# Memories a batch ahead, in the scores' visit, and turned by VectorE and a trip through HBM

## The chip, the cores and the metric

The kernel runs on one core of a Trainium2 chip. The metric is the time of one execution on the device in microseconds (us), as the median of several runs; lower is better.

## What is computed

An attention with 32 memories a head, followed by a bilinear feed-forward network, for 8 batches (0 to 7) of 8 heads, 576 positions and 64 channels. All data is float32.

```python
a = phi - max(phi, over positions)            # phi: [b, h, 576, 32]
a = exp(a); a = a / (sum(a, over positions) + 1e-9)
k_m = einsum('bhsm,bhsd->bhmd', a, k)         # the memories of the keys
v_m = einsum('bhsm,bhsd->bhmd', a, v)         # and of the values
scores = matmul(q, k_m.T) / 8
attn = softmax(scores, over the 32 memories)
x = matmul(attn, v_m)                         # 4608 rows of 512
h = (x @ w1) * (x @ w2)                       # 1024 wide
out = (h @ w3) @ w_out
```

The kernel multiplies w3 by w_out once, and each batch's value memories by w1 and w2, so that x itself is never made.

## The kernel before, in words

After a start that loads and multiplies the weights, a loop runs over the batches. Each turn has two stages, and the order of the instructions on every engine is written out by hand: tables of step names, run by `go`, each name advancing a generator by one piece.

`ab_stage(b)`, the product stage, multiplies the attention of batch b by its weights, for eight blocks f of 128 columns. Its periods p are numbered 0 to 9: a period runs seven products of one block (names q1 to q7, three matmuls of 288 columns each) and the other engines' steps on them: copies on ScalarE, hold_c22, gr0, gr1 and the seeds on VectorE, `high` on ScalarE and `low` on GpSimd. VectorE's hold_c22 of a block must be done before its last product q4 starts. At the `+` of each period stand the steps that the table `MEETS` names, all for batch b + 1: the maximum over positions (`top`, `row`: the maxima go to HBM and come back spread over all partitions as the tile all), the exponentials with positions along the free axis (`exp`, for the sums), `norm` (two small steps on VectorE: add 1e-9, reciprocal), and `less`, which subtracts the maxima from phi laid out by rows (two long and two short additions on VectorE) and takes its exponential (two on ScalarE). At the `*` of period 8 come the memories (`mem`, L262): 40 small matmuls of those rows with keys and values (L270 and L279, 32 columns of the array each) into the PSUM pair x, and two scaled copies on ScalarE into kvm.

`out_stage(b)` runs the output blocks of batch b (24 matmuls of 512 columns each, in four groups of six, written O) and, between them by the table `REST`, the rest of batch b + 1: `blocks` (L293: two transposes on TensorE with ident, and VectorE's copy into the tile memory), the scores (`sc0`, `sc1`: 8 small matmuls each), M0 directly behind them, the softmax over memories (`se`, `sn`, `pr`), the sums of the attention's blocks (`ps`), and M3, M2, M1. M0 to M3 multiply memory by a quarter of w1 and w2 each (L387), and those quarters are read back from HBM (the DRAM tiles kept) by SP: W0 to x, W1 to the tile kv2, W2 to the tile q, W3 to the tile kv0. W1 and W3 can only be issued once the memories have read keys and values from these tiles, W2 once sc1 has read the queries. The loads of the next inputs (`phi2`, `rows2`, `q2`, `kv2`) follow M1.

SP issues every DMA, in order, and all go through one queue. TensorE, ScalarE, VectorE and GpSimd each run their own list in order.

Of the kernel before, what the change touches and what calls it, by code (L numbers as in the profile page):

```python
# [8 lines left out]
F32 = mybir.dt.float32  # L9
# [30 lines left out]
A11 A6 B3 A3 norm.1 A6 A10 C24 A6 A3 B10 A10 C24 S3 A3 A7 A3 N3 A7 A10 A10 B7 N3 A10 O0 A7 less.1 N3 A7 A2 A7 A15  # L40
less.1 less.1 A2 B15 A15 A14 less.1 A15 A15 B14 A15 less.1 B2 A13 A2 A14 mem.1 A2 A14 mem.1 X1 A13 X3 A2 A14 B13 A14
blocks.1 A12 A13 A13 blocks.1 B12 A13 A12 A12 A12 A12
""".split()
MEETS = {0: "<M3 top", 1: "top row exp", 2: "exp", 3: "norm", 4: "W0", 5: "less", 6: "less less less", 7: "less"}
REST0 = """
# [10 lines left out]
def memory_attention__then__bilinear_ffn_kernel(  # L56
# [67 lines left out]
    def pair():  # L124
        x = psum_pair()
        return [x[:, i] for i in range(2)]
# [13 lines left out]
    def whole(step):  # L140
        for _ in step:
            pass
# [45 lines left out]

    ready = {}

    def attention(b):

        v = {}
# [68 lines left out]
        def memories():  # L262
            kvt = loaded.pop(("kv", b))
            v["kvm"] = att.tile([P, NT, 2 * D], F32, name="kvm")

            ps = pair()
            for t in range(NT):
                for i in range(4):
                    for h in range(4):
                        nc.tensor.matmul(  # L270
                            ps[t][h * M : (h + 1) * M, : 2 * D],
                            lhsT=v["a"][:, i, t, h * M : (h + 1) * M],
                            rhs=kvt[i][:, (4 * t + h) * 2 * D : (4 * t + h + 1) * 2 * D],
                            start=i == 0,
                            stop=False,
                        )
            for h in range(4):
                for t in range(NT):
                    nc.tensor.matmul(  # L279
                        ps[t][h * M : (h + 1) * M, : 2 * D],  # L280
                        lhsT=v["a"][t * D : (t + 1) * D, 4, 0, h * M : (h + 1) * M],
                        rhs=kvt[4][t * D : (t + 1) * D, h * 2 * D : (h + 1) * 2 * D],
                        start=False,
                        stop=True,
                    )
            yield
            for t in range(NT):

                nc.scalar.activation(
                    out=v["kvm"][:, t], in_=ps[t][:, : 2 * D], func=AF.Copy, scale=v["sm"][:, t : t + 1]  # L290
                )

        def blocks():  # L293
# [3 lines left out]
            yield  # L297
            nc.vector.tensor_copy(out=memory[b % 2], in_=ps.rearrange("p (t g m) -> p t g m", t=NT, m=M))

        def scores(n, banks):  # L300

            if "q" not in v:
                v["q"] = loaded.pop(("q", b))
                s_sb = att.tile([P, 5 * NT * P], F32, name="s_sb", tag="a")
                v["s"] = s_sb[:, : NT * S].rearrange("p (n k m) -> p n k m", n=2, m=M)
            ps = [x[:, :HALF] for x in banks()]
            turned = n == 1 and b > 0
            for g in range(NG):
                for t in range(NT):
                    nc.tensor.matmul(  # L310
                        ps[t][g * M : (g + 1) * M],
                        lhsT=memory[b % 2][t * D : (t + 1) * D, t, g],
                        rhs=v["q"][t * D : (t + 1) * D, g, n * HALF : (n + 1) * HALF],
                        start=True,
                        stop=True,
                    )
            yield
            nb = NBLK // 2
            for t in range(NT):
                nc.vector.transpose(  # L320
                    out=v["s"][:, n, (t ^ turned) * nb :][:, :nb], in_=ps[t].rearrange("p (k m) -> p k m", m=M)
                )
# [45 lines left out]
                nc.gpsimd.tensor_tensor(out=lo[:, i:j], in0=y, in1=hi[:, i:j].bitcast(F32), op=ALU.subtract)  # L368
                yield

        steps = {"ps": sums, "top": top, "row": row, "less": less, "exp": exp, "norm": norm, "mem": memories, "blocks": blocks}
        steps |= {f"turn{i}": lambda i=i: turn(i) for i in (0, 4)}
        for n in range(2):
            steps |= {f"sc{n}": lambda n=n: scores(n, banks_aa if b and n else pair)}
# [53 lines left out]
    def memory_weights(b, q):  # L428
        ps = pair() if q == 3 else [psum(ps_ab, "bab"[q]) for _ in range(NT)]
        weights_times(b, q, w12_sb[0] if (b, q) == (1, 0) else staged[q], ps)  # L430
        (b12, b11), (b21, b22) = [[x[:, k * FQ : (k + 1) * FQ] for k in range(2)] for x in ps]
        yield
        if q == 2:
            x = const.tile([P, CW], F32, name="u", bufs=2).rearrange("p (k f) -> p k f", k=4)
        else:
            x = room_of_sums()[:, int(q == 1)]
        t1, t2, t3, t4 = [x[:, k] for k in range(4)]
        mh, ml = ready["M", b][q] = [new.tile([P, 7, FQ], F32R, name=f"{z}{q}") for z in ("mh", "ml")]
        firsts = ((0, 1, b11), (1, 3, ps[1].rearrange("p (k f) -> p k f", k=2)))
        nc.scalar.copy(out=t4, in_=b12)  # L440
        for i, j, y in firsts:
            nc.scalar.copy(out=mh[:, i:j], in_=y)
        yield
        for y, p, r in ((t1, t4, b11), (t3, b22, t4), (t2, b22, t1), (t4, b21, t2)):
            nc.vector.tensor_tensor(out=y, in0=p, in1=r, op=ALU.subtract)
        for i, j, y in firsts:
            nc.vector.tensor_tensor(out=ml[:, i:j], in0=y, in1=mh[:, i:j].bitcast(F32), op=ALU.subtract)
        yield
        nc.scalar.copy(out=mh[:, 3:], in_=x)  # L449
        for k in range(0, 4, 2):  # L450
            y = slice(3 + k, 5 + k)
            nc.gpsimd.tensor_tensor(out=ml[:, y], in0=x[:, k : k + 2], in1=mh[:, y].bitcast(F32), op=ALU.subtract)  # L452
# [196 lines left out]
    def ab_matmuls(b, n, f, w):  # L649
# [12 lines left out]
            )  # L662
        yield

    POOLF = (2, 3)

    def ab_unit(b, n, f):
# [89 lines left out]

    def ab_stage(b, go, before, part):
        u = [Sevenths(b, f) for f in range(NF)]
        order = """  # L760
            0q1 0q5 0seed_u 0keep_q5 / 2gr1 + 1q7 1q3 2high * 2low 1hold_c22 1gr0 0q6 0q2 0hold_c11 0seed_c 1q4
        """.split()
        for p in range(NF + 2):
            for x in order:
                if x == "+":
                    if p == NF and b + 1 < B:
                        started[b] = out_block(b, 0), 1
                        next(started[b][0])
                    for what in MEETS.get(p, "").split():
                        if what[0] == "<":  # L770
                            before(what[1:])
                        elif what[0] == "W":
                            if b + 1 < B:
                                whole(stage(int(what[1])))
                        else:
                            go(what)
                elif x == "*":
                    if p == NF:
                        go("mem")
                        go("mem")  # L780
                        if b + 1 == B:
                            started[b] = out_block(b, 0, psum_pair()[:, 0]), 1
                            next(started[b][0])
                elif x == "/":
                    if p == 0:
                        whole(part)
                elif 0 <= p - int(x[0]) < NF:
                    getattr(u[p - int(x[0])], x[1:])()
# [44 lines left out]
    def goer(b):  # L833
        begun = {x[:-2]: step for x, step in under_way.items() if b == 0 and x.endswith(".1")}

        def go(what):
            if b + 1 == B:
                return
            if what not in begun:
                if what[0] == "M":  # L840
                    begun[what] = memory_weights(b + 1, int(what[1]))
                else:
                    begun[what] = steps[b + 1][what]()
            next(begun[what], None)
            if what == "M0" and new is None:
                renew()

        return go
# [12 lines left out]
    def out_stage(b, go):  # L861
        ready["M", b + 1] = {}
        part, left = out_parts(b), 4 * ((S + b % 2 * REST_ROWS) // P)
        if b in started:
            left -= started[b][1]
        next(part)
        for what in (REST if b else REST0) + left * ["O"]:
            if what == "O":
                if left > (b + 1 < B):
                    left -= 1  # L870
                    next(part)
            elif what[:-1] in LOADS:
                whole(load(what, b))
            elif what[0] == "W":
                if b + 1 < B:
                    whole(stage(int(what[1])))
            else:
                go(what)
        return part
# [78 lines left out]
```

## Time and profile before

| | us |
|---|---|
| median of 3 runs (509.57 to 510.89) | 509.64 |
| the profiled execution | 509.37 |
| its span, first to last instruction | 507.6 |
| TensorE busy | 502.7 |
| VectorE busy | 356.4 |
| ScalarE busy | 295.9 |
| GpSimd busy | 192.8 |
| DMA queue, share of 16 engines | 52.5% |

The profile shows one execution. Busy times of different engines overlap; the busy time of TensorE counts matmuls whose ends overlap too. What counts is who waited for whom, and the chain of waits, which goes back from the last instruction through whatever released each step.

### The profile page before, as it was taken

What the parts mean: (1) busy time and instruction counts of PE and PEld (TensorE: products, weight loads), DVE (VectorE), ACT (ScalarE), POOL (GpSimd) and SP (SyncE); (2) the same over time, 40 slices, a digit from 0 to 9 for tenths busy, and PEclk for the clock granted to TensorE, in tenths of its full rate; (3) what the DMA queues carried; (4) which work ended last, traced back from release to release, by engine and by line L of the source; (5) the groups of instructions that cost most, each with busy time, mean ns of one, the idle gap of its engine ahead of it and who ended that gap; (6) DMA issues with size and microseconds to landing.
All of it is one profiled execution on the core that took longest, in us unless ns stands there. A gap on an engine that the chain in (4) does not pass through costs nothing.

```text
span 507.6 us, 10188 instructions
## 1 busy us (share of the span) xinstructions
PE 502.7 (99%) x3879; PEld 412.0 (81%) x3879; DVE 356.4 (70%) x741; ACT 295.9 (58%) x574; POOL 192.8 (38%) x137
## 2 busy tenths in 40 slices
PE   8999999999999999999999999999999999999997
PEld 6447688967986899769977899779977898689986
DVE  5889999598758847497749576697759474976400
ACT  7998977438653756267626465377635564475411
POOL 0000010027641744238532925168515644276500
PEclk9999999999999999999999999999999999999999
DMA  8999983979216931657246730776077522500011
GB/s 344 418 416 420 393 331 110 375 251 386 99 49 240 365 111 57 235 202 284 81 177 207 321 116 1 271 297 232 2 262 260 205 94 78 215 28 16 1 47 57
DMA packets 21680, 102.24 MB, mean 201 GB/s; under 512 B 2560, under 2 KB 3712, under 8 KB 12800
## 3 DMA queue, kind: packets, MB, share of 16 engines
q1 hardware_dynamic: 21632, 101.60, 52.5%
q8 instruction: 30, 0.49, 0.4%
q14 instruction: 18, 0.15, 0.1%
HBM read 87.95 MB, written 13.64 MB: 200 GB/s over the span
## 4 chain that ended last, share of the span: by engine, by line
PE 89%; DMA 5%; DVE 3%; ACT 1%; issue 1%; POOL 0%; POOLq 0%; ACTq 0%
PE o L803 38%; PE b L688 14%; PE a L688 9%; PE o L688 9%; DMA kv<-in_weights 5%; PE x L270 3%; PE a L569 3%; PE b L569 3%; PE b L387 3%; PE x L387 2%; PE x L635 1%; PE a L387 1%; PE x L803 1%; PE b L656 1%; PE x L310 1%; PE a L656 1%
## 5 line engine op out<-in xcount | busy, mean ns | idle before, releaser
L756 POOL TENSOR_TENSOR gl<-u,gh 128x576 fp32r<-128x576 f32 x56 | 80.0, 1428 | 97.8 <-ACT gh L753 82.3
L803 PE MATMUL o<-W,gh 128*128 128x512 f32 (+1 forms) x288 | 96.4, 389 | 0.0
L452 POOL TENSOR_TENSOR ml<-x,mh 128x512 fp32r<-128x512 f32 x42 | 58.4, 1424 | 83.0 <-ACT mh L449 83.0
L688 PE MATMUL b<-ahl,mh 128*128 128x288 f32 x336 | 73.3, 299 | 0.0
L803 PEld LDWEIGHTS o<-W,gh 128*128 128x128 f32 x288 | 53.7, 188 | 16.7 <-issue 5.9
L688 PEld LDWEIGHTS b<-ahl,mh 128*128 128x128 f32 x336 | 54.5, 188 | 2.8 <-issue 1.2
L803 PE MATMUL o<-Wh,gh 128*128 128x512 f32 (+1 forms) x144 | 56.0, 389 | 0.0
L803 PE MATMUL o<-Wh,gl 128*128 128x512 f32 (+1 forms) x144 | 55.4, 385 | 0.0
L803 PE MATMUL o<-W,gl 128*128 128x512 f32 (+1 forms) x144 | 55.4, 384 | 0.0
L803 PE MATMUL o<-Wl,gh 128*128 128x512 f32 (+1 forms) x144 | 55.3, 384 | 0.0
L688 PE MATMUL b<-ahl,ml 128*128 128x288 f32 x168 | 49.6, 295 | 0.0
L688 PE MATMUL a<-ahl,mh 128*128 128x288 f32 x224 | 48.0, 296 | 0.0
L688 PE MATMUL o<-ahl,mh 128*128 128x288 f32 x224 | 48.0, 295 | 0.0
L738 DVE TENSOR_TENSOR gr<-b,a_sb 128x288 f32<-128x288 f32 x56 | 25.5, 456 | 28.5 <-PE b L688 27.7
L730 DVE TENSOR_TENSOR o<-b,a_sb 128x288 f32<-128x288 f32 x56 | 25.9, 462 | 27.4 <-PE b L688 27.4
L746 DVE TENSOR_TENSOR u<-b,gr 128x288 f32<-128x288 f32 x56 | 25.6, 458 | 25.8 <-PE b L688 25.1
L753 ACT CAST gh<-u 128x576 fp32r<-128x576 f32 x56 | 38.0, 678 | 7.8 <-DVE u L746 7.8
L707 ACT COPY b<-a 128x288 f32<-128x288 f32 x56 | 21.5, 384 | 33.6 <-DVE u L746 21.0
L813 ACT COPY osb<-o 128x512 f32<-128x512 f32 (+1 forms) x36 | 20.6, 571 | 30.7 <-PE o L803 30.7
L688 PEld LDWEIGHTS a<-ahl,mh 128*128 128x128 f32 x224 | 36.4, 188 | 0.9 <-POOL ahl L368 0.4
L688 PEld LDWEIGHTS o<-ahl,mh 128*128 128x128 f32 x224 | 36.0, 188 | 0.0
L803 PEld LDWEIGHTS o<-Wh,gh 128*128 128x128 f32 x144 | 27.0, 188 | 9.9 <-issue 5.0
(189 smaller groups left out, 1125.7 us busy)
## 6 DMA issues: line engine op xcount, KB each, us to landing
kv<-in_kv SPq DMA_DIRECT2D x16, 1024.0 KB, 10.8
kv<-kept SPq DMA_DIRECT2D x14, 1024.0 KB, 7.1
raw<-in_weights SPq DMA_DIRECT2D x10, 1024.0 KB, 13.3
q<-in_qT SPq DMA_DIRECT2D x8, 1152.0 KB, 19.6
out<-osb SPq DMA_DIRECT2D x31, 256.0 KB, 2.0
q<-kept SPq DMA_DIRECT2D x7, 1024.0 KB
raw<-in_weights SPq DMA_DIRECT2D x12, 512.0 KB, 5.5
x<-kept SPq DMA_DIRECT2D x6, 1024.0 KB
```

The costliest lines, as they stand in the source:

```text
L387: nc.tensor.matmul(ps[t][g * M : (g + 1) * M], lhsT=memory[b % 2][d, t, g], rhs=w[d, :, g], start=True, stop=True)
L452: nc.gpsimd.tensor_tensor(out=ml[:, y], in0=x[:, k : k + 2], in1=mh[:, y].bitcast(F32), op=ALU.subtract)
L569: nc.tensor.matmul(pw[r][i], lhsT=x[:, i * P : (i + 1) * P], rhs=y, start=k == 0 and j == 0, stop=k == NF - 1 and j == len(pairs) - 1,)
L688: nc.tensor.matmul(ps, lhsT=x[:, j], rhs=y[:, i], start=start and k == 0, stop=stop and k == 2, skip_group_check=True,)
L707: nc.scalar.copy(out=self.u, in_=self.a)
L730: nc.vector.tensor_tensor(out=self.c, in0=self.u, in1=self.s5, op=ALU.add)
L738: nc.vector.tensor_tensor(out=self.c22, in0=self.u, in1=self.s5, op=ALU.add)
L746: nc.vector.tensor_tensor(out=self.gr[:, 1], in0=self.u, in1=self.c22, op=ALU.mult)
L753: nc.scalar.copy(out=self.cut(gh), in_=self.gr)
L756: nc.gpsimd.tensor_tensor(out=self.cut(gl), in0=self.gr, in1=self.cut(gh).bitcast(F32), op=ALU.subtract)
L803: nc.tensor.matmul(ps, lhsT=x[f][:, at : at + P], rhs=y[f][:, cols], start=f == 0 and k == 0, stop=f == NF - 1 and k == 2,)
L813: nc.scalar.copy(out=osb[:, cols], in_=ps)
```

## The change

From batch 3 on (the fourth) the tile memory is no longer made by transposes on TensorE. A new step `flip` transposes kvm in 32x32 blocks on VectorE, writes the result to HBM with four DMAs that put the blocks in place, and reads it back into memory with a fifth. From batch 4 on the memories are made a batch ahead, in the output stage that also makes the scores of the batch before: `shared` lets both use the same PSUM pair x, the scores its first 288 columns, the memories the columns behind. The step names get a number, how many batches ahead of b they work (`mem:2`). Batch 2 is the turn between the two orders: its product stage runs the softmax over rows of batches 3 and 4, with batch 3's memories in period 5 instead of period 8, and its output stage has batch 4's memories behind the scores. In period 8 the place of the memories goes to one more group of output matmuls (`EXTRA`). Loads move along: `kv2`, `rows2` and `phi2` to the product stage of batch 2, later `phi3`, `rows3`, `kv3` in the output stages.

```diff
+FAR = 3
+MEETS_FAR = {0: "<M3 phi2 top:1", 1: "top:1 row:1 exp:1", 2: "exp:1", 3: "less:1", 4: "less:1 less:1 norm:1 less:1 less:1", 5: "mem:1 mem:1 W0 kv2 rows2 top:2", 6: "flip:1 top:2 row:2", 7: "flip:1 exp:2", 8: "exp:2 norm:2", 9: "less:2"}
+REST_LATE = """
+mem:2 sc0 sc1 M0 mem:2 W1 W3 sc0 se0 flip:2 sc1 W2 O flip:2 se0 se0 O se1 se1 se1 sn0 sn1 sn0 M0 sn1 M0 sn0 pr0 O sn1 M0 pr1 ps O
...
     ready = {}
+
+    shared = {}
...
             ps = pair()
+            if b > FAR:
+                shared["x"] = ps
+                ps = [x[:, HALF:] for x in ps]
...
+        def flip():
+            turned = big.tile([P, NT * P], F32, name="flipped", tag="all", bufs=2)
+            nc.vector.transpose(out=turned, in_=v["kvm"].rearrange("p t d -> p (t d)"))
+            kept = dram.tile([P, NT, NG, M], F32, name="flip")
+            for g in range(NG):
+                nc.sync.dma_start(
+                    out=kept[:, :, g].rearrange("(j c) t m -> c t j m", c=M),
+                    in_=turned[g * M : (g + 1) * M].rearrange("p (t j m) -> p t j m", t=NT, m=M),
+                )
+            yield
+            nc.sync.dma_start(out=memory[b % 2], in_=kept)
+            yield
...
-            ps = [x[:, :HALF] for x in banks()]
+            ps = [x[:, :HALF] for x in (shared.pop("x", None) if n == 0 else None) or banks()]
...
+    EXTRA = 1
...
+        meets = MEETS if b + 1 < FAR else MEETS_FAR if b + 1 == FAR else MEETS_LATE
...
                     if p == NF:
-                        go("mem")
-                        go("mem")
+                        if b + 1 < FAR:
+                            go("mem")
+                            go("mem")
+                        elif b + 1 < B:
+                            for _ in range(EXTRA):
+                                next(started[b][0])
+                            started[b] = started[b][0], 1 + EXTRA
...
-        for what in (REST if b else REST0) + left * ["O"]:
+        for what in (REST0 if b == 0 else REST if b + 1 < FAR else REST_FAR if b + 1 == FAR else REST_LATE) + left * ["O"]:
```

What the tables do to the order is seen at three places (in the changed file the lines stand 13 to 38 lower: L803 becomes L841, L310 L339, L387 L416, L270 L286). TensorE before, in an output stage: the transposes, six output matmuls (names W and g), the scores' two halves and M0.

```order
L803 MATMUL o<-Wl_89,gh_612 128x512
L296 MATMUL x<-ident,kvm 128x128 x2
L803 MATMUL o<-W_582,gh_613 128x512
L803 MATMUL o<-W_582,gl_621 128x512
L803 MATMUL o<-W_583,gh_613 128x512
L803 MATMUL o<-W_582,gh_614 128x512
L803 MATMUL o<-W_582,gl_622 128x512
L803 MATMUL o<-W_583,gh_614 128x512
L310 MATMUL x<-q,memory_82 32x288 x8
L310 MATMUL a<-q,memory_82 32x288 x8
L387 MATMUL b<-x,memory_82 32x512 x8
```

TensorE now, in the output stage of batch 4: the product stage's last product, batch 6's memories, the scores of batch 5 and M0.

```order
L718 MATMUL b<-ahl,ml_3382 128x288
L286 MATMUL x<-kv_3362,rows 32x128 x8
L286 MATMUL x<-kv_3364,rows 32x128 x8
L286 MATMUL x<-kv_3362,rows 32x128 x8
L286 MATMUL x<-kv_3364,rows 32x128 x8
L295 MATMUL x<-kv_3366,rows 32x128 x8
L339 MATMUL x<-q,memory_83 32x288 x8
L339 MATMUL a<-q,memory_83 32x288 x8
L416 MATMUL b<-x,memory_83 32x512 x8
```

The transposes are gone, and the memories stand against the scores with nothing between. ScalarE before, in batch 2's output stage: the scores' two exponentials (L331) with an output copy between them, then M0's copies.

```order
L753 CAST gh_616<-u 128x576
L331 ACTIVATE s_sb<-s_sb 128x576
L813 COPY osb<-o 128x512
L331 ACTIVATE s_sb<-s_sb 128x576
L440 COPY x<-b 128x256
```

ScalarE now, at the same place: batch 4's exponentials over rows (L250) stand behind the scores' first one.

```order
L783 CAST gh_616<-u 128x576
L851 COPY osb<-o 128x512
L360 ACTIVATE s_sb<-s_sb 128x576
L250 ACTIVATE rows<-rows 128x640
L250 ACTIVATE rows<-rows 128x512
L360 ACTIVATE s_sb<-s_sb 128x576
L469 COPY x<-b 128x256
```

The memories of batch 4, which read these rows, come 12 output matmuls after M0 on TensorE; before, a batch's rows were done in its product stage. SP before, from W0 to the next inputs:

```order
L424 DMA x<-kept_90 128x2048
L424 DMA kv_2446<-kept_91 128x2048
L424 DMA kv_2448<-kept_93 128x2048
L424 DMA q<-kept_92 128x2048
L817 DMA out<-osb 128x512 x2
L149 DMA ph<-in_phiT 128x1152
```

SP now, in a late stage, from W1 on:

```order
L453 DMA kv_4559<-kept_91 128x2048
L453 DMA kv_4561<-kept_93 128x2048
L321 DMA flip<-flipped 64x4x32 x4
L453 DMA q<-kept_92 128x2048
L326 DMA memory_83<-flip 128x256
L859 DMA out<-osb 64x512 x2
```

The four writes of the flip stand between W3 and W2, and the read back into memory behind W2.

## Rows read from the trace of the kernel before

**Rows 1.** The page, parts 1 and 2: TensorE's busy time, its granted clock.

```profile
PE 502.7 (99%) x3879; PEld 412.0 (81%) x3879; DVE 356.4 (70%) x741; ACT 295.9 (58%) x574; POOL 192.8 (38%) x137
...
PEclk9999999999999999999999999999999999999999
```

**Rows 2.** Waits of TensorE: who waited, for whom, total us, times, longest.

```profile
PE x L387 <- DVE w L516: 0.2, 1, 0.2
```

**Rows 3.** Chain of waits, 203 to 224 us: start us, us, what.

```profile
202.81 1.36 PE o L803 x6
204.17 0.40 PE b L688 x3
...
204.97 1.88 PE x L270 x64
...
207.24 0.60 PE b L688 x3
...
209.22 0.22 PE x L296 x2
209.44 1.40 PE o L803 x6
210.84 0.65 PE x L310 x16
...
212.82 7.07 PE o L803 x30
219.89 1.02 PE x L387 x16
```

**Rows 4.** Chain of waits, 194 to 206 us: the last product of period 6.

```profile
199.54 0.47 PE b L688 x3
```

**Rows 5.** VectorE in order of time behind the scores: start us, us, what, [idle before].

```profile
211.59 0.85 DVE L320 STREAM_TRANSPOSE s_sb<-x 128x288 f32<-128x288 f32 x2 [1.69 <-PE x L310]
...
213.90 0.72 DVE L329 TENSOR_TENSOR s_sb<-s_sb,small 128x576 f32<-128x576 f32 x1
```

**Rows 6.** VectorE in order of time in period 6 of batch 2's product stage.

```profile
197.55 0.75 DVE L230 TENSOR_TENSOR rows<-rows,all 128x512 f32<-128x512 f32 x1
198.22 0.58 DVE L234 TENSOR_TENSOR rows<-rows,all 64x128 f32<-64x128 f32 x2
198.83 0.46 DVE L738 TENSOR_TENSOR gr<-b,a_sb 128x288 f32<-128x288 f32 x1
```

**Rows 7.** Line 241 (norm's first step): duration in ns, min/median/max.

```profile
L241 DVE TENSOR_SCALAR small<-small x8: 156/984/1282, 20.7 to 409.7; 128x2 f32<-128x2 f32 x8
```

**Rows 8.** ScalarE in order of time: an exponential over rows, and the scores' exponential.

```profile
198.33 0.74 ACT L237 ACTIVATE rows<-rows 128x640 f32<-128x640 f32 x1
...
214.71 0.69 ACT L331 ACTIVATE s_sb<-s_sb 128x576 f32<-128x576 f32 x1 [5.67 <-DVE s_sb L329]
215.30 0.57 ACT L813 COPY osb<-o 128x512 f32<-128x512 f32 x1
```

**Rows 9.** SP's issues in order of time: start us, us, what.

```profile
206.92 0.79 SPq L424 DMA_DIRECT2D kv<-kept  x2
...
236.85 1.15 SPq L219 DMA_DIRECT2D mx<-turned  x4
238.90 0.34 SPq L221 DMA_DIRECT2D all<-mx  x1
```

**Rows 10.** The page, part 6: DMA issues, KB each, median us from issue to landing.

```profile
kv<-kept SPq DMA_DIRECT2D x14, 1024.0 KB, 7.1
...
all<-mx SPq DMA_DIRECT2D x7, 128.0 KB, 3.0
```

**Rows 11.** Stretches: length, busy us by engine (instructions), clock, DMA share, GB/s.

```profile
500.16:500.87 0.71, 0.71 (x9) 0.71 (x8) 0.00 (x0) 0.00 (x0) 0.00 (x0) 1.00 0.95 369
266.00:268.00 2.00, 2.00 (x10) 1.63 (x9) 1.97 (x5) 0.69 (x2) 0.00 (x0) 1.00 1.01 381
...
217.50:218.50 1.00, 1.00 (x6) 0.85 (x5) 0.73 (x6) 0.31 (x1) 0.00 (x0) 1.00 0.11 43
```

More of the change, by code (lines that the diff above doesn't have):

```diff
@@ L42 @@
 blocks.1 A12 A13 A13 blocks.1 B12 A13 A12 A12 A12 A12
+""".split()
+FAR = 3
+MEETS_FAR = {0: "<M3 phi2 top:1", 1: "top:1 row:1 exp:1", 2: "exp:1", 3: "less:1", 4: "less:1 less:1 norm:1 less:1 less:1", 5: "mem:1 mem:1 W0 kv2 rows2 top:2", 6: "flip:1 top:2 row:2", 7: "flip:1 exp:2", 8: "exp:2 norm:2", 9: "less:2"}
+MEETS_LATE = {0: "<M3 top:2", 1: "top:2 row:2 exp:2", 2: "exp:2", 3: "norm:2", 4: "W0", 5: "less:2", 6: "less:2 less:2 less:2", 7: "less:2"}
+REST_FAR = """
+O sc0 sc1 M0 sc0 se0 sc1 W2 less:2 se0 less:2 O se0 less:2 less:2 se1 se1 se1 sn0 sn1 sn0 M0 sn1 M0 sn0 O mem:2 mem:2 W1 W3 pr0 sn1 M0 pr1 O ps O
+O O O flip:2 flip:2 M3 M2 M1 phi3 rows3 q2 O kv3 ps M1 M2 M3 ps M1 O M2 M2 M1 M3 O O M3
+""".split()
+REST_LATE = """
+mem:2 sc0 sc1 M0 mem:2 W1 W3 sc0 se0 flip:2 sc1 W2 O flip:2 se0 se0 O se1 se1 se1 sn0 sn1 sn0 M0 sn1 M0 sn0 pr0 O sn1 M0 pr1 ps O
+O O M3 M2 M1 phi3 rows3 q2 O kv3 M1 ps M2 M3 M1 ps O M2 M2 M1 M3 O O M3
 """.split()
@@ L369, in sums @@
                 yield
-        steps = {"ps": sums, "top": top, "row": row, "less": less, "exp": exp, "norm": norm, "mem": memories, "blocks": blocks}
+        steps = {"ps": sums, "top": top, "row": row, "less": less, "exp": exp, "norm": norm, "mem": memories, "blocks": blocks, "flip": flip}
         steps |= {f"turn{i}": lambda i=i: turn(i) for i in (0, 4)}
@@ L768, in ab_stage @@
                         next(started[b][0])
-                    for what in MEETS.get(p, "").split():
+                    for what in meets.get(p, "").split():
                         if what[0] == "<":
                             before(what[1:])
+                        elif what[:-1] in LOADS:
+                            whole(load(what, b))
                         elif what[0] == "W":
@@ L836, in go @@
         def go(what):
-            if b + 1 == B:
+            name, _, ahead = what.partition(":")
+            ahead = b + int(ahead or 1)
+            if ahead >= B:
                 return
@@ L840, in go @@
                 if what[0] == "M":
-                    begun[what] = memory_weights(b + 1, int(what[1]))
+                    begun[what] = memory_weights(ahead, int(what[1]))
                 else:
-                    begun[what] = steps[b + 1][what]()
+                    begun[what] = steps[ahead][name]()
             next(begun[what], None)
```

## The prediction, written before the changed kernel ran

> **What bounds the kernel now.** I read the page first. TensorE is busy for 502.7 of 507.6 us, and its granted clock is nine tenths or more in all 40 slices [rows 1], the 2.4 GHz level. Then the waits of TensorE: after the start it waited for another engine once, for 0.2 us [rows 2]. Then the chain of waits: from 86 us on it lies on TensorE, and its section for batch 3 shows piece after piece of a stage touching the next [rows 3]. So the time is the sum of TensorE's instructions. An instruction taken from it is time gained, a wait put on it is time lost, and whatever the other engines do costs nothing until TensorE waits for it. The question is two sums: what the change takes from TensorE, and where it makes it wait.
>
> **What it removes: the transposes.** A batch's two transposes (L296) take 0.22 us of the chain, and the six output matmuls behind them 1.40 us where others take 1.36 [rows 3]: 0.25 us a batch. In the new order they are gone for batches 3 to 7, five times: 1.2 us gained. VectorE's copy of the result into memory goes with them.
>
> **What it moves: the memories.** They take 2.27 us (204.97 to 207.24), and the three matmuls after them 0.60 us where three take 0.40 [rows 3]: going back from narrow tiles to whole ones costs 0.20 us. For batches 5, 6 and 7 the memories now stand directly ahead of the scores, which are in narrow tiles too, so one way back is saved each time: 0.6 us. Batches 3 and 4 keep a visit of their own (in period 5 of batch 2's product stage, and among its output blocks), at the same price. Together **1.8 us** less work on TensorE.
>
> **What the turn costs elsewhere.** Per batch one 128x256 transpose on VectorE (two of 128x288 take 0.85 us, so 0.42 [rows 5]), four writes and a read on SP's queue, 128 KB each way. From batch 4 on its result is wanted a batch later, so the trip itself is covered. What is not covered is where the trip and the moved steps stand in line. Five places:
>
> 1. *Product stage of batch 2, periods 4 and 6.* This stage carries the softmax over rows of two batches. In period 6 before, the second long and the two short additions (197.55 to 198.83 us) stand ahead of VectorE's hold_c22 [rows 6], and the product that waits for it takes 0.47 us instead of 0.40 [rows 3, 4]: the cover is just used up. In period 4 now the same additions are followed by norm's two small steps, 0.16 us each at the least [rows 7], so hold_c22 is 0.33 us later and TensorE waits about 0.40. With norm's median of 0.98 for the first step it would be 1.2. In period 6 now stand the flip (0.42), a maximum and a small transpose, about as much as the 1.28 us that cost 0.07: 0.1. Together **0.5** (0.1 to 1.3). The memories in period 5 keep the delay from piling up.
>
> 2. *Batch 4's memories wait for their weights.* In batch 2's output stage they come 12 output matmuls after the scores' visit; one visit lasts 1.98 us (210.84 to 212.82) and 30 outputs 7.07 (to 219.89) [rows 3], so TensorE gets there 4.8 us after the scores begin. They need the exponentials over rows, which stand on ScalarE behind the scores' first exponential. VectorE before: transposes 0.75 us after the scores begin, the subtraction at 3.06 [rows 3, 5]. Now an addition of 0.67 [rows 6] comes first: subtraction at 3.73, done 0.72 later at 4.45; ScalarE starts 0.09 after that, goes on after 0.59, and the first exponential over rows takes 0.74 [rows 8]: done at 5.87. TensorE waits **1.0 us**. The second one is shorter and is needed only by the later memories matmuls, so it adds nothing.
>
> 3. *The data of batch 4's row maxima.* In period 5 SP issues 2880 KB (keys, values, rows) as batch 3's memories let go of the tiles. Two loads of 1024 KB, issued within 0.79 us, landed 7.1 us after the second's issue [rows 9, 10], some 7.5 in all; 832 KB more at about 380 GB/s [rows 11] make it 9.7. The first tile is free before the memories' last quarter, some 0.8 us before their end. Then the last of the maxima goes out (238.0 us to 238.9 until the broadcast is issued [rows 9], with 0.3 for its own issue) and comes back in 3.0 [rows 10]; the first addition takes 0.67. That is 13.8 us after the memories. TensorE reaches the scores after 66 product and 18 output matmuls, 8.8 + 4.1 us, and wants VectorE 0.75 later: 13.65. This is the edge, so I charge **0.3** (0 to 2): VectorE is late by it, and point 2 by the same.
>
> 4. *Weights for M3 in batch 2's output stage.* W1 and W3 are issued when the memories release the tiles, 0.32 us before their end at 207.24, and W3 lands about 7.2 after that end [rows 3, 9, 10]. Before, M3 came 12.65 us after it (219.89); now after 30 outputs, 7.07. TensorE waits **0.1** (0 to 1).
>
> 5. *Weights for M2 in the output stages of batches 3 to 5.* SP now issues W1, W3, the four flip writes, then W2. M2 comes 1.98 + 8.43 + 1.02 = 11.4 us after the memories (visit, 36 outputs, M3). Before, that traffic had ebbed at about 217.6 us [rows 11], 10.4 after them; with the landing some 0.8 us is left for the flip's 1024 packets of 128 B, 64 on each DMA engine. No row shows such a burst. By bytes it is 0.35 us. At the price of the output's 2 KB packets (0.95 share at 369 GB/s, 84 ns each [rows 11]) it is 5.4. From 8 KB packets (1.01 at 381 GB/s, 347 ns) to 2 KB the price goes with the bytes, so I take 0.5: covered, and I charge **0.1** a batch for the spread of landings, 0.3 in all (0 to 14).
>
> The Trainium skill, page DMA: Bandwidth & Descriptors, section Specifications, speaks against point 5: full rate asks for at least 512 B a transfer, and below that the engine reads, modifies and writes. It gives no time for it; by it the price would lie toward the upper end, and the sum would come out as the second rival below. No row of the trace decides between the two.
>
> **The sum.** 1.8 less, and 0.5 + 1.0 + 0.3 + 0.1 + 0.3 = 2.2 more: 0.4 us more. The profiled execution took 509.37 us, 507.6 of it the span; that gives 509.8. The median of the runs, 509.64, is 0.27 above it, so the forecast for a median is **510.0 us**. A measurement of this kernel can tell about 0.3%, 1.5 us, from no change.
>
> **Rivals.** *The waits stay away.* Points 1, 3 and 4 lie at the edge of their cover, and so tight a kernel has run with one wait; if point 2 is milder as well, only the gain is left: 509.64 - 1.8 = 507.8. Against it: point 2 is a full microsecond, from rows with little play. *M2 becomes the bound.* The mechanism is W2 behind the small packets on SP's queue, in three stages. It decides once 64 packets take over 0.8 us, 13 ns each, and makes the kernel measurably slower from about 1.3 us, 20 ns each. At half the upper price, 2.7 us, each M2 waits 1.9: 5.7 us in place of 0.3, 515.4. For it: such packets are new here, and many; against it: the price that went with the bytes. *Batch 2's loads are late.* If the 2880 KB take 2 us longer, since the flip's and the maxima's packets stand behind them, points 3 and 2 grow by that much and the scores themselves may wait for memory: 512. *The change saves less than it says:* if memories ahead of the scores still pay for the change of tiles, 0.6 us is not gained: 510.6, inside the forecast.
>
> **How the numbers follow.** The forecast has a chance of 0.50 (its own range, 508.5 to 511.2, lies within 0.3%); the waits stay away 0.18 (faster); M2 becomes the bound 0.18 (slower); late loads 0.14, of which 0.10 slower and 0.04 within 0.3%. Faster by over 0.3%: 0.18; within: 0.54; slower: 0.28. The range goes from 508.0, which leaves out about a tenth where every wait stays away, to 514.0, which leaves out the worse half of the M2 case.
>
> **What would show it.** Right: five pairs of L296 fewer; the memories of batches 5 to 7 touching the scores in the chain; a wait of TensorE of about 1 us for ScalarE's rows in batch 2's output stage; a late hold_c22 in its product stage; waits for q<-kept of a few tenths at most. Wrong: waits of TensorE for a weight load of over 1 us in batches 3 to 5 (second rival), exponentials over rows that are ready when batch 4's memories come (first), scores that wait for memory (third). It would also be wrong if the granted clock fell in one of the new waits; before, it never did [rows 1].

## The result, and where the time went

The changed kernel takes **517.73 us** in the median of four runs (516.06 to 519.22), the kernel before 510.0 beside it: a ratio of 1.0142, interval 1.0122 to 1.0162. That is 7.7 us more where 0.4 was forecast, and outside the range. The profiled execution is the longest one, 519.22 us, 9.85 above that of before. Its page:

```profile
PE 502.0 (97%) x3869; PEld 411.7 (80%) x3869; DVE 355.1 (69%) x741; ACT 296.0 (57%) x574; POOL 193.6 (37%) x137
...
PEclk9999999999999998999999999999999999999999
```

TensorE issues ten instructions fewer than in [rows 1], the five pairs of transposes, and is busy for 97% of the span where it was 99%; its clock has one slice below nine tenths. The waits of TensorE (line, whom it waited for: total us, times, longest; those in the start left out), where before there was one of 0.2 us [rows 2]:

```profile
PE b L718 <- DVE gr L768: 3.2, 2, 2.5
PE b L416 <- DMA q<-kept: 2.5, 3, 1.4
...
PE x L416 <- DMA kv<-kept: 1.2, 1, 1.2
PE x L339 <- DMA memory<-flip: 1.2, 1, 1.2
PE x L286 <- ACT rows L250: 0.8, 1, 0.8
```

(Line numbers moved: products L718, scores L339, M0 to M3 L416, memories L286, hold_c22 L768.) Each has a place.

**At 192 us, batch 2's product stage: 2.5 us, and 1.7 more by the clock.** The chain of waits (start, us, what) leaves TensorE for the trip of batch 3's row maxima, their writes to HBM and the broadcast:

```profile
186.56 2.58 DMA mx<-turned
189.29 4.61 DMA all<-mx
194.60 0.46 DVE gr L768
195.10 0.72 PE b L718 x3
```

VectorE reaches the first long addition at 190.7 us, finds the broadcast `all` not landed, and stands there for 3.3 us with hold_c22 behind it. When TensorE goes on, the three matmuls of a product take 0.72 us instead of 0.40. The stretches (length, busy us of five engines, granted clock, DMA share, GB/s) tell why:

```profile
192.30:195.10 2.80, 0.26 (x2) 0.03 (x1) 1.11 (x3) 0.00 (x0) 1.26 (x1) 1.00 0.85 327
...
195.60:198.80 3.20, 3.20 (x16) 3.20 (x15) 2.52 (x8) 2.18 (x6) 0.00 (x0) 0.50 0.01 5
```

Behind 2.8 us with hardly a matmul the granted clock is 0.50, the 1.2 GHz level, for 3.2 us: half of that, 1.6, is lost, and 0.1 at its edge. The four executions lie 3 us apart, and their mean granted clock goes with it: 0.999 in the shortest, 0.996 in the longest.

**At 216 us: the scores wait 1.2 us for memory.** SP's issues (start, us, what) in the stage before:

```profile
202.39 0.81 SPq L171 DMA_DIRECT2D kv<-in_kv  x2
203.25 1.27 SPq L176 DMA_DIRECT2D kv<-in_kv  x1
204.58 0.65 SPq L188 DMA_DIRECT2D rows<-in_phi  x1
206.22 2.66 SPq L321 DMA_DIRECT2D flip<-flipped  x4
208.98 3.60 SPq L232 DMA_DIRECT2D mx<-turned  x4
213.70 0.34 SPq L234 DMA_DIRECT2D all<-mx  x1
214.15 0.37 SPq L326 DMA_DIRECT2D memory<-flip  x1
```

Two things show. A flip write takes 0.66 us to issue, a write of the maxima some 0.29 with its gap [rows 9]. And the four writes of the maxima take 3.6 us here where they took 1.15 there: the trace puts three waits among them, 2.5 us in all, down to `kv<-in_kv` and `rows<-in_phi`, with which they share no data. In the chain the last of them goes out when the rows have landed:

```profile
204.58 7.76 DMA rows<-in_phi
212.35 1.21 DMA mx<-turned
```

The load of the rows was issued eight places ahead of that write. At 249.87 us the chain shows the same for the first load of keys and values and the write eight places behind it. So a write seems to wait for the transfer eight places ahead; the count is read off these places, and no run varied it. The read back into memory stands behind all that.

**At 222, 232 and 260 us.** Batch 4's memories wait for ScalarE's exponentials over rows (0.8), M3 for W3 (1.2; W3 landed 8.1 us after its issue), and in batch 3's product stage hold_c22 once more stands behind an addition whose broadcast is late (0.7).

**In batches 3 to 5: M2 waits for W2.** TensorE and SP in batch 3:

```profile
283.53 1.09 PE L416 MATMUL x<-kv,memory 64*32 64x512 f32 x16
285.34 1.21 PE L416 MATMUL b<-q,memory 64*32 64x512 f32 x16 [0.73 <-DMA q<-kept]
286.20 1.21 PE L416 MATMUL a<-kv,memory 64*32 64x512 f32 x16
287.35 0.50 PE L841 MATMUL o<-Wh,gh 128*128 128x512 f32 x1
```

```profile
273.06 0.80 SPq L453 DMA_DIRECT2D kv<-kept  x2
276.65 3.23 SPq L321 DMA_DIRECT2D flip<-flipped  x4
279.98 0.55 SPq L453 DMA_DIRECT2D q<-kept  x1
```

The visit of M3, M2 and M1 takes 3.82 us (283.53 to 287.35), in batches 4 and 5 3.43 and 4.52; before, the same three visits took 2.94, 2.82 and 2.82. That is 3.2 more. SP, after W1 and W3, stood until VectorE had turned kvm (276.6) and then spent 3.2 us on issuing four writes; only then did W2 go out, and it landed 5.2 us later.

**The sum.** The list comes to 2.5 + 1.7 + 1.2 + 0.8 + 1.2 + 0.7 + 3.2 = 11.3 us. Less the 1.8 us of work gained that is 9.5, close to the 9.85 between the two profiled executions, but in part by luck. Batch 0's visit of M3, long before the first changed step, already begins 1.37 us later (chains before and now):

```profile
112.42 1.02 PE x L387 x16
113.79 1.02 PE x L416 x16
```

In the start of this execution TensorE waited 1.7 us for VectorE. Such waits are 0.2 to 1.7 us in the profiles of the changed kernels and absent from the one profile of before, and no run shows why. From that visit on the changed kernel takes 8.4 us more. Batches 2 and 6 have a shorter visit of M3, M2 and M1 than before (2.74 each, where it was 3.17 and 2.81), which takes 0.5 off: 9.0 is explained where 8.4 was measured.

**The packets were not it.** Batch 4's flip, in a stretch of 3.1 us (234.9 to 238) in which no large packet moved (1024 packets are the flip's data, the other 64 are not identified):

```profile
DMA packets 1088, 0.13 MB, mean 42 GB/s; under 512 B 1088, under 2 KB 1088, under 8 KB 1088
...
q1 hardware_dynamic: 1088, 0.13, 25.2%
```

A quarter of 16 engines for 3.1 us is 12.5 us of engine time for 1088 packets: **11.5 ns each**, 0.74 us for the 64 on an engine. That is twice the price by bytes, and less than the 13 ns from which they would have decided. This is their price with the engines else idle; what they cost beside other traffic is tested below, by writing them twice.

### The profile page after: what moved, and what is told of

Same layout as the page of the kernel before. It is cut to its first block, busy times and chain, and to the rows that moved or that the text cites. A ratio compares the mean times of both kernels' runs of the same rounds, so it can differ in the third digit from the quotient of the medians.

```text
span 517.4 us, 10209 instructions
## 1 busy us (share of the span) xinstructions
PE 502.0 (97%) x3869; PEld 411.7 (80%) x3869; DVE 355.1 (69%) x741; ACT 296.0 (57%) x574; POOL 193.6 (37%) x137
## 4 chain that ended last, share of the span: by engine, by line
PE 70%; DMA 19%; DVE 4%; ACT 3%; SPq 2%; issue 1%; DVEq 0%; ACTq 0%
PE o L841 29%; PE b L718 11%; PE o L718 7%; PE a L718 7%; DMA kv<-in_weights 5%; DMA q<-kept 3%; PE x L286 3%; DMA kv<-in_kv 2%; PE b L685 2%; PE b L416 2%; DMA all<-mx 2%; PE a L685 2%; DMA raw<-in_weights 2%; DMA mx<-turned 2%; DMA kv<-kept 2%; DMA rows<-in_phi 1%
## 5 line engine op out<-in xcount | busy, mean ns | idle before, releaser
L841 PE MATMUL o<-W,gh 128*128 128x512 f32 (+1 forms) x288 | 95.4, 388 | 0.0
L718 PE MATMUL b<-ahl,mh 128*128 128x288 f32 x336 | 73.2, 299 | 3.2 <-DVE gr L768 3.2
L841 PEld LDWEIGHTS o<-W,gh 128*128 128x128 f32 x288 | 53.7, 188 | 17.7 <-issue 6.7
L718 PEld LDWEIGHTS b<-ahl,mh 128*128 128x128 f32 x336 | 55.3, 190 | 5.8 <-DVE gr L768 3.7
L841 PE MATMUL o<-Wh,gh 128*128 128x512 f32 (+1 forms) x144 | 56.0, 389 | 0.0
L841 PE MATMUL o<-Wh,gl 128*128 128x512 f32 (+1 forms) x144 | 55.3, 384 | 0.0
L841 PE MATMUL o<-Wl,gh 128*128 128x512 f32 (+1 forms) x144 | 55.3, 384 | 0.0
L841 PE MATMUL o<-W,gl 128*128 128x512 f32 (+1 forms) x144 | 55.3, 384 | 0.0
L718 PE MATMUL b<-ahl,ml 128*128 128x288 f32 x168 | 49.8, 297 | 0.0
L718 PE MATMUL o<-ahl,mh 128*128 128x288 f32 x224 | 48.5, 298 | 0.0
L718 PE MATMUL a<-ahl,mh 128*128 128x288 f32 x224 | 48.3, 297 | 0.0
L768 DVE TENSOR_TENSOR gr<-b,a_sb 128x288 f32<-128x288 f32 x56 | 25.5, 455 | 32.2 <-PE b L718 31.8
L764 ACT COPY gr<-a 128x288 f32<-128x288 f32 x56 | 22.4, 401 | 26.7 <-PE a L718 20.1
L718 PEld LDWEIGHTS a<-ahl,mh 128*128 128x128 f32 x224 | 36.6, 189 | 0.9 <-POOL ahl L397 0.4
L718 PEld LDWEIGHTS o<-ahl,mh 128*128 128x128 f32 x224 | 36.5, 190 | 0.0
## 6 DMA issues: line engine op xcount, KB each, us to landing
raw<-in_weights SPq DMA_DIRECT2D x12, 512.0 KB
```

What stands on the lines that cost most here:

```text
L718: nc.tensor.matmul(ps, lhsT=x[:, j], rhs=y[:, i], start=start and k == 0, stop=stop and k == 2, skip_group_check=True,)
L764: nc.scalar.copy(out=self.c11, in_=self.a)
L768: nc.vector.tensor_tensor(out=self.c22, in0=self.u, in1=self.s5, op=ALU.add)
L841: nc.tensor.matmul(ps, lhsT=x[f][:, at : at + P], rhs=y[f][:, cols], start=f == 0 and k == 0, stop=f == NF - 1 and k == 2,)
```

## The experiments

Each is the changed kernel with an edit in its tables; one also writes the flip twice. In the short diffs a `-` or `+` line is a piece of a table. "Before" ran beside each on the same chip (510.0 to 510.6 us).

### W2 ahead of the flip

```diff
 REST_LATE
-W1 W3 sc0 se0 flip:2 sc1 W2 O flip:2
+W1 W3 sc0 se0 sc1 W2 flip:2 O flip:2
```

> The changed kernel with one edit: in the output stages of batches 3 to 5, W2 is issued ahead of the flip's four writes. In the changed kernel TensorE lost 1.08, 0.69 and 1.79 us there on M2, while SP waited for VectorE's turn (until 276.65 us in batch 3) and then spent 3.2 us on issuing the four writes, W2 behind them. Theory (SP's queue in order): the waits for q<-kept fall below 0.3 us each and the time by 3.0 to 3.6, to about 514.3; the flip's own read still comes in time, since it is wanted a stage later. Rival (the 1024 small packets fill the DMA engines, wherever they stand): W2 still lands late beside them, or the loads behind the flip do, and less than 1.5 us is won.

515.33 us (514.81 to 516.02), 2.4 less, between the two forecasts. Two of TensorE's waits:

```profile
PE o L718 <- ACT osb L851: 1.5, 1, 1.5
...
PE b L416 <- DMA q<-kept: 0.2, 1, 0.2
```

M2's wait is gone but for 0.2 us, with every packet still there: it was SP's order. Part of it came back: the flip's read now held up SP until 283.4 us, the next loads and an output followed late, and a copy for which the output's buffer was not free cost 1.5 us a stage later.

### TensorE's transposes in the new order

```diff
-flip
+blocks        (wherever it stands)
```

> The changed kernel with its new order of the memories kept, but turned by TensorE's transposes and VectorE's copy, as before the change; no trip through HBM. Theory (the trip and its place on SP's queue cost most): the waits for M2 (3.6), for memory<-flip (1.2) and for the addition at 260 us (0.75) go, the transposes come back (5 x 0.25): 517.7 - 5.5 + 1.2 = 513.4. The waits for the maxima in batch 2's product stage, for ScalarE's rows and for M3 stay. Rival (the moved memories cost most, the trip little): 517 or more.

515.48 us (513.35 to 516.14): 2.2 less, not 4.3. The waits for M2, for memory<-flip and at 260 us are all gone, as expected. But the maxima's wait was 3.1 us in this profile (it varies from 2.0 to 3.1), with the slow clock behind it, and the transposes waited 1.2 us for VectorE. So neither forecast alone: in the changed kernel's profile the waits that go with the trip come to 5.1 us, the moved steps cost the rest.

### The load ahead of the maxima

```diff
 MEETS_FAR
-0: "<M3 phi2 top:1", 1: "top:1 row:1 exp:1"
+0: "<M3 top:1", 1: "top:1 row:1 phi2 exp:1"
```

> The changed kernel with one load moved: in batch 2's product stage the load of 576 KB for batch 4's maxima is issued behind batch 3's maxima and not ahead of them. Theory (the maxima's way through HBM is late, and that load ahead of it makes it so): the broadcast lands about 2 us earlier, TensorE's wait for hold_c22 falls from 2.6 us to under 1, the granted clock no longer falls behind it (1.7 us), and the time is about 514. Rival (the addition simply stands two periods too early, and VectorE would wait as long without the load): under 1 us is won, 516.7 or more.

515.3 us, from 512.43 to 519.68, a spread too wide to tell the forecasts apart by the time. In the profile the broadcast landed 1.8 us earlier, and TensorE's wait is still 2.0 us:

```profile
192.15 1.57 DVE L243 TENSOR_TENSOR rows<-rows,all 128x512 f32<-128x512 f32 x1 [1.88 <-DMA all<-mx]
```

VectorE still waited 1.9 us for it, and the addition itself took 1.57 us, where 0.69 is usual. So the load made the trip later, but it was too late without the load ahead of it, as the rival had said: from the first write (185.27 us) to VectorE's start it still took 6.9 us. Of the 2.0 us some 0.9 is the long addition.

### The maxima made earlier

```diff
 REST (batch 1)
-M2 M2 M1 M3 O O M3
+M2 M2 M1 M3 O O M3 top:2 top:2 row:2
 MEETS_FAR
-0: "<M3 phi2 top:1", 1: "top:1 row:1 exp:1"
+0: "<M3 phi2", 1: "exp:1"
```

> The changed kernel with one step moved: batch 3's row maxima and their trip through HBM are made at the end of batch 1's output stage and not in periods 0 and 1 of batch 2's product stage; the addition that waits for them stays in period 3. Theory (in the changed kernel that addition stands two periods too early for the trip, and VectorE, which runs in order, holds up TensorE behind it): the wait for hold_c22 at 192 us (2.0 to 3.3 us in four profiles) falls below 0.5, no run shows a lower granted clock behind it, and the time is 517.7 - 2.6 - about 1 = 514, with less spread. Rival (the slow part is the addition beside GpSimd's work, 1.57 us in one profile against 0.69): over 1 us of the wait stays.

514.82 us (513.15 to 517.88), 2.9 less. The wait goes with the trip's start:

```profile
PE b L416 <- DMA q<-kept: 3.5, 3, 2.4
...
PE b L718 <- DVE gr L768: 0.2, 1, 0.2
```

The rival falls too: the addition took 1.50 us in this profile, and the wait went all the same. The spread stayed, though: M2's wait reached 2.4 us here, and the clock fell behind that.

### Batch 2's loads

```diff
 MEETS_FAR
-5: "mem:1 mem:1 W0 kv2 rows2 top:2", 6: "flip:1 top:2 row:2", 7: "flip:1 exp:2"
+5: "mem:1 mem:1 W0 top:2", 6: "flip:1 top:2 row:2", 7: "flip:1 rows2 kv2 exp:2"
 REST_FAR
-pr0 sn1 M0 pr1 O ps O O O O flip:2 flip:2 M3
+pr0 sn1 M0 pr1 flip:2 O ps O O O O O flip:2 M3
```

> The changed kernel with batch 2's stages reordered on SP: keys, values and rows of batch 4 (2880 KB) are issued behind the flip's read and the maxima's trip of batch 4, not ahead; in its output stage batch 4's flip comes 30 output matmuls earlier and M3 six output matmuls later. Theory (SP's queue in order, eight transfers under way): the scores' wait for memory<-flip (1.2 us), M3's wait (1.3) and the wait for the addition at 260 us (0.75) go: about 514.5. Rival (the loads are then late themselves): batch 4's additions or memories wait for rows<-in_phi or kv<-in_kv for 2 us or more, and nothing is won.

521.02 us (520.1 to 525.16), slower than the changed kernel by 3.3. The three waits it aimed at are gone, and others came:

```profile
216.51 1.69 DVE L243 TENSOR_TENSOR rows<-rows,all 128x512 f32<-128x512 f32 x1 [1.14 <-DMA rows<-in_phi]
```

```profile
PE x L286 <- ACT rows L250: 1.9, 1, 1.9
PE a L718 <- POOL ahl L397: 1.7, 1, 1.7
PE a L718 <- ACT ahl L396: 1.6, 1, 1.6
```

The rows now came 1.1 us late to their addition: the rival's mechanism, at half the size that it named, and the memories behind it waited 1.9 us where it was 0.8. The 3.3 us on ahl (the attention and its sums, split by ScalarE and GpSimd into the high and low parts that the products read) are explained further below. The clock fell as well: its mean is 0.987 in this execution. With the rows loaded where they were, only keys and values behind the read, and in REST_FAR the flip's second step behind the next loads (`O kv3` made `kv3 flip:2`):

> The changed kernel with batch 2's stages reordered on SP, mended after the reordering that made VectorE wait for its rows: the rows of batch 4 (576 KB) are issued where they were, its keys and values (2304 KB) behind the flip's read of batch 3. In its output stage batch 4's flip is written right after the weights' loads and read behind the next batch's loads, and M3 comes six output matmuls later. Theory (transfers in SP's order): the scores' wait for memory<-flip (1.2 us), M3's wait (1.3) and the wait for the addition in batch 3's product stage (0.75) go; 517.7 - 3.2 = 514.5. Rival (any order only moves the wait): batch 4's memories wait for kv<-in_kv, or the scores still for memory, by over 1 us.

515.68 us (514.4 to 517.24). No wait for memory<-flip, M3 or the addition at 260 us is left; 0.5 on ahl is new. The profiled execution, 514.4, fits the forecast. Two others took 516.9 and 517.24, and no profile shows what they lost: the maxima's wait is kept in this kernel, and their mean clock is 0.997 and 0.996, but one of 514.46 has 0.996 as well.

### All of them together

The maxima made earlier, batch 2's loads and flip in this last order, W2 ahead of the flip, and the flip's reads of batches 4 to 7 behind the next loads (`kv3 M1 flip:2`):

> The changed kernel with the moves together: the maxima of batch 3 made earlier, keys and values of batch 4 behind the flip's read, M3 of batch 2 six output matmuls later, W2 ahead of the flip's writes in batches 3 to 5, and every read of the flip from batch 4 on behind the next batch's loads. The flip, its packets and the moved memories are all kept. Theory (the losses are steps that stand in the wrong place of SP's and VectorE's order; the trip itself costs TensorE nothing): what is left is the gain of 1.8 us and the wait for ScalarE's rows, 0.9: about 508.6, at or below the kernel before. Rival (small packets or the number of transfers cost the loads time wherever they stand): 511 or more, with waits for loads in batches 3 to 5.

511.32 us (511.07 to 512.43), ratio 1.0033 (1.002 to 1.0046): 6.4 of the 7.7 us are back. By the number, and by its waits for a load in batches 3 to 5, this is the rival's outcome (511 or more), but that small packets were its cause had still to be settled. Left are 0.8 for ScalarE's rows, 0.5 on ahl, and 1.5 for W2. W1, W3 and W2 follow each other without a gap, 3 MB, and M2 comes 2.3 us sooner behind the memories than in the kernel before, where the last three matmuls of a product, two transposes and one group of outputs more stood between [rows 3]. So the weights were put in the order in which they are wanted, and batch 4's memories one group of outputs later:

```diff
 REST_LATE
-W1 W3 sc0 se0 sc1 W2 flip:2
+W3 sc0 se0 sc1 W2 W1 flip:2
 REST_FAR
-O mem:2 mem:2 W1 W3 pr0 sn1 M0 pr1 flip:2 O ps O O O O O M3 ... q2 kv3
+O O mem:2 mem:2 W3 W1 pr0 sn1 M0 pr1 O ps flip:2 O O O O M3 ... q2 O kv3
```

> The kernel with all moves, mended where it still lost: in the output stages from batch 2 on the weights are loaded in the order in which they are wanted (W3, W2, W1, not W1, W3, W2), and batch 4's memories come six output matmuls later, its flip behind the scores' sums. Theory (M2's rest of 0.9 and 1.0 us was 3 MB of weights at some 400 GB/s, of which the first was not yet wanted; the memories' 0.8 us was ScalarE's exponentials): all of these go, and the gain of 1.8 us is left: 508.4 to 508.8, a ratio of about 0.997. Rival (the small packets hold up whatever is on the queues): a wait of 0.5 us or more for W1 or W2 stays in at least two of the three stages.

512.38 us (511.7 to 513.33), no better. Every wait for weights and rows is gone, with all the packets and transfers still there: what the last run had left was the order of the weights, not the packets. But ahl costs 1.6 + 1.7 us and the clock behind. ScalarE in order of time:

```profile
222.93 0.59 ACT L851 COPY osb<-o 128x512 f32<-128x512 f32 x1 [0.37 <-PE o L841]
231.38 0.59 ACT L851 COPY osb<-o 128x512 f32<-128x512 f32 x1 [7.86 <-PE o L841]
231.86 1.16 ACT L396 CAST ahl<-sums 128x1152 fp32r<-128x1152 f32 x1
```

One group of outputs more (the `O` of `O kv3`) had moved ahead of the cast, and with it the copy of the next finished output block: ScalarE stood 7.9 us for TensorE's block, the cast that TensorE wants behind it. The slower reordering above had the same order. Two variants of this kernel ran beside it, both with that flaw: TensorE's transposes for the flip, and each flip write of batches 4 to 7 made twice.

> The same kernel with the memories turned by TensorE's transposes and VectorE's copy and no flip. If the turn on VectorE through HBM is worth what the prediction gave it, this is 1.2 us slower than the kernel with all moves and the flip (five times 0.25); if the small packets and transfers still cost something there, it is equal or faster.

515.71 us (514.52 to 516.89), 3.3 more: the 1.25 of the transposes, and two waits that the flip has not, 1.2 us of the transposes for VectorE's steps on the scores and 0.7 of M0 to M3 for VectorE's copy into memory. Those two belong to where the transposes were put, and no other place was tried.

> The kernel with all moves and the flip, whose writes of batches 4 to 7 are each made twice, the second time to a place that nobody reads: four times 1024 more packets of 128 B, and four times some 2.5 us more of SP's time. If the flip stands where nothing waits for it, the time stays within 0.5 us; if small packets cost 80 ns each, as by bytes and shares the largest row of before allowed, each stage loses up to 5 us and the time rises by over 5.

512.93 us (512.33 to 514.4), 0.55 more, and the intervals of the two ratios overlap (1.0043 to 1.007, and 1.0029 to 1.0056). 4096 more small packets cost next to nothing where nobody stands behind them: the forecast of the dear packets, over 5 us, is out.

With one output block put back (`O kv3` to `kv3`):

> The kernel with all moves and the weights in the order of use, with one output block of batch 2 put back: in the run before, one block more stood ahead of ScalarE's first cast of ahl, which therefore waited for TensorE's block, and TensorE lost 1.7 and 1.9 us at the start of batch 3's product stage and ran at the lower granted clock behind them. Theory (every loss was an order, no part of the trip itself): those go, no wait over 0.3 us is left after 86 us, and the time is that of before less the 1.8 us of work: 508.3 to 508.8, a ratio of 0.995 to 0.998. Rival (there is always a next wait): 510 or more, with a new wait of over 1 us.

508.84 us (508.03 to 511.99), ratio 0.9985 (0.9969 to 1.0002). Nine of twelve executions lie at 508.0 to 510.1, three at 511.3 to 512.0, with a mean clock of 0.996 to 0.997 where the others have 0.999 or 1. The one new wait is the addition at 253 us, 0.6. SP:

```profile
228.11 2.56 SPq L321 DMA_DIRECT2D flip<-flipped  x4
...
232.81 0.97 SPq L171 DMA_DIRECT2D kv<-in_kv  x2
...
240.72 4.30 SPq L232 DMA_DIRECT2D mx<-turned  x4
```

The flip held up the loads, and two of the maxima's writes waited 3.3 us for keys and values, the loads eight places ahead: 4.3 us where 1.15 is usual. The profile is of a short execution; what the three long ones lost is not shown. So the turn was put earlier on VectorE (`pr0 flip:2 sn1` for `ps flip:2`):

> The last kernel with one step moved: batch 4's turn on VectorE in batch 2's output stage stands 3 us earlier among the scores' steps, so that SP issues its four writes, and the loads behind them, by so much earlier. In the run before, SP waited for that turn until 228.1 us, the next batch's loads followed late, two of the four writes of batch 4's successor's maxima waited for those loads (the eighth transfer ahead of each), and the addition behind them cost TensorE 0.7 us at 253 us; in 3 of 12 executions it cost about 3 us with the lower clock. Theory: that wait goes, the slow executions with it, and the time is 508.0 to 508.5, faster than the kernel before by 0.3 to 0.45%. Rival (the spread has another cause): the median stays at 508.8, with a quarter of the executions at 511 or more.

**508.05 us** (507.42 to 508.63), ratio **0.9958** (0.9944 to 0.9971): faster than the kernel before. None of its five executions lies apart from the rest; with a quarter apart, as in the last run, that would happen about one time in four, so it is not shown that the long ones are gone. All waits of TensorE in it, of which only the one on ahl lies behind the start, and two rows of its chain:

```profile
PE x L664 <- POOL ident masks.py:199: 1.4, 1, 1.4
PE a L598 <- DVE wo L545: 0.6, 2, 0.5
PE a L718 <- POOL ahl L397: 0.5, 1, 0.5
PE x L416 <- DVE s_sb L349: 0.2, 1, 0.2
PE x L416 <- DVE w L545: 0.2, 1, 0.2
```

```profile
263.36 1.88 PE x L286 x64
265.62 0.48 PE x L339 x16
```

The profiled execution took 507.87 us, 1.5 less than that of before, though it lost 0.7 in the start. From batch 0's visit of M3 on it is 2.2 us shorter, with 0.5 of waiting left: 2.7 were gained. 0.9 of that is in the visits of M3, M2 and M1 in batches 2 to 6, which take 2.74 us here and took 3.17, 2.94, 2.82, 2.82 and 2.81 before; what held those up is not shown. The rest is the 1.8 that was forecast. SP issues the maxima's writes in 1.15 us again:

```profile
224.53 2.55 SPq L321 DMA_DIRECT2D flip<-flipped  x4
...
240.84 1.15 SPq L232 DMA_DIRECT2D mx<-turned  x4
```

## The prediction, point by point

**The steps that failed.** The sum put waits of 2.2 us on TensorE, and the profile shows 11.3, the slower clock included. Two terms make most of the difference: point 1 (0.5, measured 4.2), which left out that an addition waits for a trip through HBM, and point 5 (0.3, measured 3.2), which wrote down SP's order without its times.

**What it removes and moves: right.** Ten instructions of TensorE fewer, and the scores' visit joined to the memories: in the last kernel the first scores take 0.48 us behind the memories, against the 0.65 of [rows 3]. The 1.8 us are what the well-ordered version gained, besides 0.9 in visits that the prediction took to be free of waits before. The rival that the joint visit would still pay for the tiles falls.

**Point 1 failed most: 0.5 forecast, 4.2 measured.** It counted only VectorE's busy time in front of hold_c22, in periods 4 and 6, where the list shows no wait now. The wait came in period 3: the addition there also waits for a trip, and the prediction had that trip's rows and used them for batch 4 alone: writes to broadcast 2.05 us, broadcast to landing 3.0 [rows 9, 10], 5.05 in all. From the first write at 185.67 that is 190.72, and the addition stood at 190.7: no slack by these rows alone. Measured was more, 194.0 with the load of 576 KB ahead of the trip, and 6.9 us of trip with that load behind it. The new table leaves two periods between `row` and `less` where the old left four. Moving the trip alone took the wait away. The clock's 1.7 us were named as a way to be wrong and had no price.

**Point 2 held:** 1.0 forecast, 0.8 measured, by the mechanism described.

**Point 3 and the third rival: 0.3 forecast, 1.2 measured; the place was right, the cause half.** The range said that loads ahead of the maxima would make VectorE late; VectorE's addition did wait. What TensorE met first was memory, whose read stands behind the maxima's on SP. The rival allowed for that and said 512. That small writes wait for big loads they have nothing to do with was in no term.

**Point 4:** 0.1 forecast, up to 1; measured 1.2, and 1.5 or 1.6 in four other profiles. The landing of 7.1 us was a median; at M3 it was 8.1.

**Point 5 and the second rival: right place, wrong cause.** M2 did become a bound, 3.2 us in place of 0.3, and the rival's 515.4 is nearer than the forecast. But its mechanism, packets dearer than 13 ns, did not occur: a packet took 11.5, and twice as many moved the time by 0.55 us. What failed is the line before: SP issues "W1, W3, the four flip writes, then W2" was written down as an order without times. Waiting for VectorE's turn and 0.65 us an issue put W2 out at 279.98, 7 us after W1, and W2 needs about 5 to land.

The Trainium skill, page DMA: Bandwidth & Descriptors, section Measured (under Bandwidth), gives about 10.5 ns a packet as a minimum, for loads that GpSimd issues; the 11.5 ns of these writes, which SP issues, lie close to it. With the 512 B that the prediction quoted from the Trainium skill (that page, section Specifications) the trace agrees so far that packets of 128 B cost twice their price by bytes; whether the engine reads, modifies and writes is not shown, and the cost was too small here to matter.

**Not seen at all:** the addition at 260 us (0.7), late because the flip of batch 4 held up the loads behind it, and a write of the maxima the broadcast; with the loads ahead of the flip's read the wait was gone.

## What to carry to other kernels

When a step moves on a queue that runs in order, write its whole trip as a line of times (source ready, issue time of each part, landing, reader) and compare the end with the reader's place; busy time in front of the reader is only one of the terms, and a wait in front of it on the issuing queue held up all that followed it (here 7 us between W1 and W2). A change whose gain is a fraction of a per cent lives or dies by such places: the same steps were 1.4% slower than before in one order and 0.4% faster in another. And where TensorE waits, price its clock too: here it added 1.7 us to a wait of 2.5.

## What the runs showed of the hardware

- In the changed kernel, issuing a 32 KB write that falls into 256 packets of 128 B takes SP 0.6 to 0.67 us; a reload of weights, 1024 KB in 128 pieces of 8 KB, 0.32 to 0.55; a write of 256 B in two pieces some 0.25. In these rows the time goes with the number of pieces, not with the bytes.
- A 128 B packet to HBM cost a DMA engine 11.5 ns, in the stretch of batch 4's flip.
- TensorE's clock stood at 0.50 for 3.2 us behind 2.8 us with hardly a matmul; behind waits of 2.0, 2.0 and 2.1 us in three profiles it stayed at 1.00.
- One long addition on VectorE took from 0.69 to 1.76 us. In five profiles an operation of GpSimd was under way when it began (additions of 1.10, 1.50, 1.57, 1.69 and 1.76 us), and each of the five ended 0.54 to 0.56 us after that operation; beside the 0.69 GpSimd had just finished. So the addition seems to stand while GpSimd works; no run took GpSimd's operation away.
